# Splitting the first loads of a DCN cross network over three DMA queues

## The chip, the cores and the metric

The kernel runs on one core of one Trainium2 chip. The metric is the device time of one execution in microseconds (us), lower is better; the time before is the median of 3 runs.

## The reference

Six layers of a cross network over a batch of 4096 rows with 416 features, all in bfloat16:

```python
B, F, D, L = 4096, 26, 16, 6
Din = min(F * D, 1024)            # 416
# x0: (B, Din), ws: (L, Din, Din), bs: (L, Din)
def reference(x0, ws, bs):
    x = x0
    for l in range(ws.shape[0]):
        x = x0 * (x @ ws[l] + bs[l]) + x
    return x
```

## The kernel before

The batch is worked on in four blocks of 1024 rows (index `s`), each through six layers (index `l`). Inside a block everything is transposed: features lie on the partitions, rows on the free axis. The 416 features are three full chunks of 128 (`c`, `m`, `k`) and a tail of 32. The block's 1024 columns are two halves of 512 (`h`), so that layer `l` of half 0 can leave PSUM while half 1 is being multiplied. The sum over layers is not added by a vector engine: the products of all layers of a block pile up in the same PSUM banks, since x of layer l is x0 times (1 + the sum so far), and the running bias sum `cb_sb` takes the place of the bias.

For each layer TensorE does, in this order: the main matmuls of half 0 (`main`, 36 matmuls of 128 x 32 weights by 512 columns, four of them beside each other in the array), the tail's contribution to the three chunks and to the tail itself (`tail_rows`, which uses the weights `wt_sb` and, for the tail by tail corner of 32 x 32, the tile `wc_sb`), the contribution of the chunks to the tail (`tail_outs`), and the main matmuls of half 1. VectorE takes each finished bank to bfloat16 (`leave`, L429, six in every layer). The tail goes through ScalarE (L439), a multiplication on GpSimd (L452) and four copies that swap quarters, two on ScalarE (L416) and two on GpSimd (L418).

The corner tile `wc_sb` is zero but for 32 x 32 blocks. It is set to zero once (L272, GpSimd), and `corner` (L274) copies the blocks out of `wt_sb` on GpSimd: layer 0's before the loops (L541), layer 1's after the first layer's tail (L571), those of layers 2 to 5 after the second's (L573).

The start is written out by hand. Fourteen matmuls on constants (`fill`, L293) run while the first rows are loaded. The first half of block 0, four tiles of 128 rows (`xin_sb`), is transposed on TensorE with the identity `ident` (L500), two tiles and one chunk at a time, and copied from PSUM by VectorE (L515, chunks 0 and 2) and ScalarE (L510, chunk 1) into `x0T_sb`. The second half of block 0 comes by a transposing DMA (`load_transposed`, L205), like the later blocks. Layer 0's first half runs chunk by chunk (`k` outermost), so that each chunk of its weights W0 is needed only when its turn comes; in between stand the bias sums (`bias_sums`, from the biases `bsa_sb` and the triangular mask `u_sb`) and the transposing of the tail's rows (`tail_in`, from `xin_sb` and `xtl_sb`).

The DMA queues are filled ahead of all else, in program order: SyncE issues rows 0 to 255, the three chunks of W0, the tail columns `xtl_sb`, the transposing load, W1, the tail weights of layer 1 (`wt1`), W2, the tail weights of layers 2 to 5 (`wt2`), W3 to W5, and the later blocks. ScalarE issues rows 256 to 511, the biases and layer 0's tail weights (`wt0`). GpSimd issues none.

A small planner (`Plan`) keeps, for each key such as `("w", 1)` or `("wc", ...)`, who wrote and who read it last, and turns that into semaphore waits. The order of instructions on an engine is the order in which they are added. GpSimd's copies that move data between partitions carry `shifts=True`, and the key `("shift",)` keeps them apart from GpSimd's other work.

Of the kernel before, what the change touches and what calls it, by code (L numbers as in the profile page):

```python
# [15 lines left out]
class Plan:  # L16
# [11 lines left out]
    def add(self, eng, fn, reads=(), writes=(), adds=(), parts=(), dma=None, shifts=False):  # L28
        if eng == "gpsimd" and dma is None:
            if shifts:  # L30
                adds = tuple(adds) + (("shift",),)
            else:
                reads = tuple(reads) + (("shift",),)
        op = Op()
        op.eng, op.fn, op.marked, op.dma, op.waits = eng, fn, False, dma, []
        needs = []
        for key in tuple(reads) + tuple(adds):
            needs += [(w, True) for w in self.writer.get(key, ())]
            if key[0] == "ps":
                needs += [(r, False) for r in self.readers.get(key, ())]  # L40
        for key in tuple(writes) + tuple(adds):
            needs += [(w, True) for w in self.writer.get(key, ())]
            needs += [(r, False) for r in self.readers.get(key, ())]
        for key in parts:
            needs += [(r, False) for r in self.readers.get(key, ())]
        clock = self.clock[eng]
        for need, raw in sorted(needs, key=lambda n: -n[0].idx):
            lane = need.group if need.dma else need.eng
            if dma and need.dma == dma:
                continue  # L50
            if need.dma is None and need.eng == eng and dma is None and (eng == "tensor" or not raw):
                continue
            if clock.get(lane, -1) >= need.idx:
                continue
            op.waits.append(need)
            need.marked = True
            for lane2, idx in need.clock.items():
                clock[lane2] = max(clock.get(lane2, -1), idx)
            clock[lane] = max(clock.get(lane, -1), need.idx)
        op.idx = len(self.ops[eng])  # L60
        op.group = None
        if dma:
            op.group = ("dma", dma)
            members = self.groups.setdefault(op.group, [])
            members.append(op)
            op.marked = True
        op.clock = dict(clock)
        self.ops[eng].append(op)
        for key in reads:
            self.readers.setdefault(key, []).append(op)  # L70
        for key in parts:
            if self.readers.get(key):
                self.writer[key], self.readers[key] = [], []
            self.writer.setdefault(key, []).append(op)
        for key in tuple(writes) + tuple(adds):
# [43 lines left out]
def bass_standalone__dcn_v2_cross__recsys_kernel(  # L119
# [6 lines left out]
    B, D = x0.shape  # L126
    L = ws.shape[0]
# [14 lines left out]
    with ExitStack() as es:  # L142
# [38 lines left out]
        def quad(q):  # L181
            return slice(32 * q, 32 * q + 32)
# [8 lines left out]
        def load_main(l):  # L191
            load(
                "sync", w_sb[:, l, :, :], ws[l, 0:DF, :].rearrange("(k p) n -> p k n", p=128), "w%d" % l, [("w", l)]
            )

        def load_rows(queue, i):
            load(queue, xin_sb[:, 2 * i:2 * i + 2, :], x0_v[:, 2 * i:2 * i + 2, :], "xin%d" % i, [("xin", i)])

        def load_tail_weights(a, b, name):
            for q in range(4):  # L200
# [25 lines left out]
                part(g, 0, 1)  # L226
                part(g, 1, 1)

        load_rows("sync", 0)
        load_rows("scalar", 1)  # L230
        for k in CH:
            load("sync", w_sb[:, 0, k, :], ws[0, 128 * k:128 * k + 128, :], "w0_%d" % k, [("w", 0, k)])
        load("scalar", bsa_sb[1:L + 1, :], bs[:, :], "bs", [("bs",)])
        load(
            "scalar", wt_sb[:, 0, :], ws[0, DF:D, :].unsqueeze(0).to_broadcast([4, DR, D]), "wt0", [("wt", "wt0")]
        )
        load("sync", xtl_sb[:, 4:JS, :], x0_v[:, 4:JS, DF:D], "xtl0", [("xtl", 0)])
        load_transposed(0, H, SB)
        load_main(1)
        load_tail_weights(1, 2, "wt1")  # L240
        load_main(2)
        load_tail_weights(2, L, "wt2")
# [3 lines left out]
        for s in range(1, NS):  # L246
# [16 lines left out]
            ), reads=[("ones",)], writes=[("ident",)],  # L263
        )
        P.add("gpsimd", lambda e: e.memset(bsa_sb[0:1, :], 1.0), writes=[("bs1",)])
        P.add(
            "gpsimd", lambda e: e.affine_select(
                out=u_sb[:, :], in_=ones_sb[0:L + 1, 0:L], pattern=[[1, L]],
                compare_op=ALU.is_ge, fill=0.0, base=1, channel_multiplier=-1,
            ), reads=[("ones",)], writes=[("u",)],  # L270
        )
        P.add("gpsimd", lambda e: e.memset(wc_sb[:, :, :, :], 0.0), writes=[("wc", "wt%d" % i) for i in range(3)])  # L272

        def corner(a, b, name):  # L274
            for g in range(4):
                p = quad(g | 1)
                P.add(
                    "gpsimd", lambda e, p=p, g=g: e.tensor_copy(  # L278
                        out=wc_sb[p, a:b, g % 2, quad(g)], in_=wt_sb[p, a:b, DF:D]
                    ), reads=[("wt", name), ("wc", name)], writes=[("wc", name, g)], shifts=True,  # L280
                )


# [47 lines left out]
        def tail_rows(s, l, start):  # L331
# [22 lines left out]
            def second(pe):  # L354
# [11 lines left out]

            P.add("tensor", first, reads=keys, adds=[("ps", bank(h, m)) for h in HALVES for m in range(2)])
            P.add(
                "tensor", second, reads=keys + [("wc", wkey(l), g) for g in range(4)],
                adds=[("ps", bank(h, 2)) for h in HALVES] + [("ps", T_BANK[h]) for h in HALVES],  # L370
            )

# [17 lines left out]
        def tail_in():  # L390
# [9 lines left out]
                            )  # L400
                return ins

            P.add("tensor", fn, reads=[("ident",), ("xtl", 0), ("xin", 0), ("xin", 1)], adds=[("ps", 7)])
# [86 lines left out]

        HEAD_BANKS = ((3, 4, 5), (6, 2, 7))
        B_BANK = 6
        fill(14)
        for i in range(2):
            for c in CH:
                b = HEAD_BANKS[i][c]

                def fn(pe, i=i, c=c, b=b):
                    for j in range(2):
                        ins = pe.transpose(  # L500
                            out=psT[:, b, j * 128:(j + 1) * 128],
                            in_=xin_sb[:, 2 * i + j, c * 128:(c + 1) * 128], identity=ident[:, :],
                        )
                    return ins

                P.add("tensor", fn, reads=[("xin", i), ("ident",)], adds=[("ps", b)])
                dst, src = x0T_sb[:, c, i * 256:(i + 1) * 256], psT[:, b, 0:256]
                if c == 1:
                    P.add(
                        "scalar", lambda e, d=dst, s=src: e.activation(out=d, in_=s, func=ACTF.Copy),  # L510
                        reads=[("ps", b)], writes=[("x0Tp", c, i)],
# [216 lines left out]
```

## Time and profile before

| | |
|---|---|
| median of 3 runs | 129.5 us (129.32 to 129.96) |
| profiled execution, own time | 130.31 us |
| its span | 128.7 us |
| TensorE (PE) busy | 124.5 us, 97% of the span |
| VectorE (DVE) busy | 98.3 us, 76% |
| ScalarE (ACT) busy | 44.3 us, 34% |
| GpSimd (POOL) busy | 39.6 us, 31% |
| W0, a third each (SyncE's queue) | 104 KB, landed 3.6 us after issue (median) |
| W1 to W5, each (SyncE's queue) | 312 KB, landed 4.4 us after issue (median) |

The span runs from the first to the last instruction of the profiled execution. PE is TensorE's matmul, PEld its weight load, DVE VectorE, ACT ScalarE, POOL GpSimd; SPq and ACTq are the DMA-issuing sides of SyncE and ScalarE. L285 is line 285 of the kernel; as it stands in the helper `mm`, nearly all matmuls carry it, and the tiles behind it tell them apart. In a timeline row the first number is the start in us, the second the length in us, and the brackets give the idle time before it and what ended it. Matmuls overlap in the array, so that steps between their starts say more than their lengths.

### The profile page before, as it was taken

How to read it: one execution, taken by the hardware profiler on the slowest of the kernel's cores; microseconds unless marked ns; L12 is line 12 of the kernel's file. 1: busy time of each engine (PE TensorE's matmuls, PEld its weight loads, DVE VectorE, ACT ScalarE, POOL GpSimd, SP SyncE). 2: the span in 40 equal slices, each digit the busy share in tenths (PEclk: the TensorE clock that was granted, in tenths of full speed). 3: DMA queues.
4: the chain of work that ended last, by engine and by line, in shares of the span. 5: the costliest groups of instructions: out<-in, count | busy, mean ns of one | idle time of the engine just before them, and what ended most of it. 6: DMA issues, size and time to landing. Idle time of an engine off the chain costs nothing.

```text
span 128.7 us, 5290 instructions
## 1 busy us (share of the span) xinstructions
PE 124.5 (97%) x2402; PEld 64.5 (50%) x2402; DVE 98.3 (76%) x150; ACT 44.3 (34%) x97; POOL 39.6 (31%) x88
## 2 busy tenths in 40 slices
PE   7998999999999999999999999999999999999991
PEld 5553545545545545545545545545455455455660
DVE  0319489698797797797797797797797797797973
ACT  1525233343313243252222252252222252253920
POOL 7024273142122243242221251341320341440550
PEclk9999999999999999999999999999999999999999
DMA  3987999019999994500009407200008906100017
GB/s 110 198 203 184 265 210 231 21 37 233 195 177 240 172 166 157 156 8 5 0 5 189 81 0 248 63 5 0 0 5 167 103 5 216 54 0 5 0 38 232
DMA packets 34998, 14.11 MB, mean 110 GB/s; under 512 B 25690, under 2 KB 34976, under 8 KB 34976
## 3 DMA queue, kind: packets, MB, share of 16 engines
q1 hardware_dynamic: 34272, 13.24, 49.3%
q10 hardware_dynamic: 704, 0.54, 1.3%
q8 instruction: 19, 0.31, 1.0%
q14 instruction: 3, 0.02, 0.2%
HBM read 3.87 MB, written 3.41 MB: 57 GB/s over the span
## 4 chain that ended last, share of the span: by engine, by line
PE 88%; SPq 4%; DMA 4%; DVE 0%; issue 0%
PE ps L285 88%; DMA w_sb<-in_ws_dram 4%; SPq L205 2%; SPq L189 2%; DVE o_sb L659 0%
## 5 line engine op out<-in xcount | busy, mean ns | idle before, releaser
L429 DVE SCALAR_TENSOR_TENSOR xT_sb<-ps,cb_sb,x0T_sb 128x512 bf16<-128x512 f32 x120 | 80.9, 743 | 20.3 <-PE ps L285 20.3
L285 PE MATMUL ps<-xT_sb,w_sb 128*32 128x512 bf16 (+1 forms) x1596 | 84.2, 364 | 0.6 <-DMA w_sb<-in_ws_dram 0.6
L285 PEld LDWEIGHTS ps<-xT_sb,w_sb 128*32 128x32 bf16 x1596 | 40.8, 97 | 38.1 <-issue 4.0
L439 ACT ACTIVATE t_sb<-ps,cb_sb 64x256 f32<-64x256 f32 x46 | 21.6, 469 | 57.7 <-PE ps L285 57.4
L452 POOL TENSOR_TENSOR xt_sb<-t_sb,x0t_sb 128x256 bf16<-128x256 f32 x20 | 13.4, 672 | 63.4 <-ACT t_sb L439 63.4
L416 ACT ACTIVATE xt_sb<-xt_sb 32x256 bf16<-32x256 bf16 x38 | 15.7, 414 | 15.4 <-POOL xt_sb L452 15.2
L285 PE MATMUL ps<-x0T_sb,w_sb 128*32 128x512 bf16 (+1 forms) x336 | 19.3, 373 | 0.0
L418 POOL COPY xt_sb<-xt_sb 32x256 bf16<-32x256 bf16 x38 | 14.9, 392 | 2.4
L429 DVE SCALAR_TENSOR_TENSOR xo_sb<-ps,cb_sb,x0T_sb 128x512 bf16<-128x512 f32 x18 | 12.1, 744 | 2.5 <-PE ps L285 2.5
L285 PEld LDWEIGHTS ps<-x0T_sb,w_sb 128*32 128x32 bf16 x336 | 8.4, 98 | 7.6 <-issue 0.8
L285 PE MATMUL ps<-xt_sb,wt_sb 32*128 32x512 bf16 (+1 forms) x152 | 11.7, 326 | 0.0
L285 PE MATMUL ps<-xt_sb,wc_sb 32*128 32x256 bf16 x76 | 7.4, 268 | 0.0
L285 PEld LDWEIGHTS ps<-xt_sb,wt_sb 32*128 32x128 bf16 x152 | 2.4, 91 | 8.3 <-DVE xT_sb L429 6.4
L452 POOL TENSOR_TENSOR xot_sb<-t_sb,x0t_sb 128x256 bf16<-128x256 f32 x3 | 2.0, 672 | 9.9 <-ACT t_sb L439 9.9
L285 PE MATMUL ps<-w_sb,xT_sb 128*32 128x416 bf16 (+1 forms) x60 | 5.1, 339 | 0.0
L278 POOL COPY wc_sb<-wt_sb 32x32 bf16<-32x32 bf16 (+1 forms) x12 | 2.8, 233 | 5.1 <-DMA wt_sb<-in_ws_dram 4.5
L659 DVE TENSOR_TENSOR o_sb<-ps,xr_sb 128x416 bf16<-128x416 f32 x6 | 3.4, 587 | 1.3 <-PE ps L285 1.0
L293 PE MATMUL ps<-const-bfloat16-1.0 128*128 128x256 bf16 x14 | 3.1, 415 | 0.8 <-PEq L713 0.8
L285 PEld LDWEIGHTS ps<-xt_sb,wc_sb 32*128 32x128 bf16 x76 | 3.8, 93 | 0.2
L515 DVE COPY x0T_sb<-ps 128x256 bf16<-128x256 bf16 x4 | 1.1, 292 | 3.5 <-PE ps L500 3.2
L461 ACT ACTIVATE sS_sb<-ps,cb_sb 128x512 bf16<-128x512 f32 x5 | 3.0, 692 | 0.0
L285 PEld LDWEIGHTS ps<-w_sb,xT_sb 128*32 128x32 bf16 (+1 forms) x60 | 2.3, 97 | 1.4 <-issue 0.2
(39 smaller groups left out, 28.8 us busy)
## 6 DMA issues: line engine op xcount, KB each, us to landing
out_dram<-o_sb SPq DMA_DIRECT2D x3, 832.0 KB, 4.2
w_sb<-in_ws_dram SPq DMA_DIRECT2D x5, 312.0 KB, 4.4
xr_sb<-in_x_dram SPq DMA_DIRECT2D x1, 832.0 KB, 6.3
wt_sb<-in_ws_dram SPq DMA_DIRECT2D x4, 104.0 KB, 2.9
out_dram<-o_sb SPq DMA_DIRECT2D x2, 208.0 KB, 2.2
w_sb<-in_ws_dram SPq DMA_DIRECT2D x3, 104.0 KB, 3.6
xin_sb<-in_x_dram SPq DMA_DIRECT2D x1, 208.0 KB, 3.0
xin_sb<-in_x_dram ACTq DMA_DIRECT2D x1, 208.0 KB, 3.3
```

Source lines behind the costliest of these rows:

```text
L189: P.add(queue, lambda e: e.dma_start(dst, src), writes=writes, dma=name)
L205: "sync", lambda e: e.dma_start_transpose(x0T_sb[:, :, s * SB + a:s * SB + b], x0[s * SB + a:s * SB + b, 0:DF]),
L278: "gpsimd", lambda e, p=p, g=g: e.tensor_copy(out=wc_sb[p, a:b, g % 2, quad(g)], in_=wt_sb[p, a:b, DF:D]), reads=[("wt", name), ("wc", nam ...
L285: return pe.matmul(dst, lhsT=lhsT, rhs=rhs, start=start, stop=True, skip_group_check=True, tile_position=pos,)
L293: ins = pe.matmul(ps[:, 7, 0:256], lhsT=const[:, 0:128], rhs=const, start=True, stop=True)
L416: fn = lambda e, d=dst, s=src: e.activation(out=d, in_=s, func=ACTF.Copy)
L418: fn = lambda e, d=dst, s=src: e.tensor_copy(out=d, in_=s)
L429: "vector", lambda e: e.scalar_tensor_tensor(out=dst, in0=ps[:, bank(h, c), :], scalar=cb_sb[:, c, l:l + 1], in1=x0T_sb[:, c, o:o + H], op ...
L439: "scalar", lambda e, p=p, h=h: e.activation(out=dst[p, :], in_=ps[p, T_BANK[h], 0:G], func=ACTF.Identity, bias=cb_sb[p, NC, l:l + 1]), re ...
L452: "gpsimd", lambda e: e.tensor_tensor(out=dst, in0=t, in1=x0t_sb[:, s, 0, :], op=ALU.mult),
L461: fn = lambda e: e.activation(out=o, in_=i, func=ACTF.Identity, bias=b)
L659: "vector", lambda e: e.tensor_tensor(out=o_sb[:, jj, :], in0=ps[:, b, 0:D], in1=xr_sb[:, j, :], op=ALU.mult), reads=[("ps", b), ("xr",)], ...
```

## The change

The rows 0 to 255 become two loads of one tile each on SyncE's queue, and the start transposes tile by tile, with 12 fill matmuls and not 14. Of the first pair of tiles VectorE now copies all three chunks; of the second, ScalarE still copies chunk 1. The third chunk of W0 and all of W1 move to ScalarE's queue. The biases are loaded by GpSimd's queue. The corner blocks of layers 1 to 5 are loaded from memory by four DMAs on GpSimd's queue, each 32 partitions by 5 layers by 32 elements, and the copies after layers 0 and 1 go; layer 0's corner is still copied by GpSimd. The zeros of `wc_sb` are written by VectorE. In the planner, a shifting GpSimd copy now also waits for GpSimd's own earlier readers of the `("shift",)` key.

```diff
-            needs += [(r, False) for r in self.readers.get(key, ())]
+            needs += [(r, key == ("shift",)) for r in self.readers.get(key, ())]
...
-        load_rows("sync", 0)
-        load_rows("scalar", 1)
+        load_rows("sync", 0, 1)
+        load_rows("scalar", 2, 4)
+        load_rows("sync", 1, 2)
         for k in CH:
-            load("sync", w_sb[:, 0, k, :], ws[0, 128 * k:128 * k + 128, :], "w0_%d" % k, [("w", 0, k)])
-        load("scalar", bsa_sb[1:L + 1, :], bs[:, :], "bs", [("bs",)])
+            load(
+                ("sync", "sync", "scalar")[k], w_sb[:, 0, k, :], ws[0, 128 * k:128 * k + 128, :], "w0_%d" % k, [("w", 0, k)]
+            )
         load(
             "scalar", wt_sb[:, 0, :], ws[0, DF:D, :].unsqueeze(0).to_broadcast([4, DR, D]), "wt0", [("wt", "wt0")]
         )
+        load_main(1, "scalar")
         load("sync", xtl_sb[:, 4:JS, :], x0_v[:, 4:JS, DF:D], "xtl0", [("xtl", 0)])
         load_transposed(0, H, SB)
-        load_main(1)
         load_tail_weights(1, 2, "wt1")
...
         P.add("gpsimd", lambda e: e.memset(bsa_sb[0:1, :], 1.0), writes=[("bs1",)])
+        P.add("gpsimd", lambda e: e.dma_start(bsa_sb[1:L + 1, :], bs[:, :]), writes=[("bs",)], dma="bs")
...
-        P.add("gpsimd", lambda e: e.memset(wc_sb[:, :, :, :], 0.0), writes=[("wc", "wt%d" % i) for i in range(3)])
-
-        def corner(a, b, name):
+        P.add("vector", lambda e: e.memset(wc_sb[:, :, :, :], 0.0), writes=[("wc",)])
+        for g in range(4):
+            P.add(
+                "gpsimd", lambda e, g=g: e.dma_start(
+                    wc_sb[quad(g | 1), 1:L, g % 2, quad(g)], ws[1:L, DF:D, DF:D].rearrange("l p n -> p l n")
+                ), reads=[("wc",)], writes=[("wc1",)], dma="wc",
+            )
+
+        def corner():
             for g in range(4):
                 p = quad(g | 1)
                 P.add(
-                    "gpsimd", lambda e, p=p, g=g: e.tensor_copy(
-                        out=wc_sb[p, a:b, g % 2, quad(g)], in_=wt_sb[p, a:b, DF:D]
-                    ), reads=[("wt", name), ("wc", name)], writes=[("wc", name, g)], shifts=True,
+                    "gpsimd", lambda e, p=p, g=g: e.tensor_copy(out=wc_sb[p, 0, g % 2, quad(g)], in_=wt_sb[p, 0, DF:D]),
+                    reads=[("wt", "wt0"), ("wc",)], writes=[("wc0", g)], shifts=True,
                 )
...
-                "tensor", second, reads=keys + [("wc", wkey(l), g) for g in range(4)],
+                "tensor", second, reads=keys + ([("wc1",)] if l else [("wc0", g) for g in range(4)]),
...
-        fill(14)
-        for i in range(2):
+        fill(12)
+        for j in range(4):
+            i, r = divmod(j, 2)
             for c in CH:
                 b = HEAD_BANKS[i][c]
-
-                def fn(pe, i=i, c=c, b=b):
-                    for j in range(2):
-                        ins = pe.transpose(
-                            out=psT[:, b, j * 128:(j + 1) * 128],
-                            in_=xin_sb[:, 2 * i + j, c * 128:(c + 1) * 128], identity=ident[:, :],
-                        )
-                    return ins
-
-                P.add("tensor", fn, reads=[("xin", i), ("ident",)], adds=[("ps", b)])
+                P.add(
+                    "tensor", lambda pe, j=j, r=r, c=c, b=b: pe.transpose(
+                        out=psT[:, b, r * 128:(r + 1) * 128], in_=xin_sb[:, j, c * 128:(c + 1) * 128], identity=ident[:, :]
+                    ), reads=[("xin", j), ("ident",)], adds=[("ps", b)],
+                )
+                if r == 0:
+                    continue
                 dst, src = x0T_sb[:, c, i * 256:(i + 1) * 256], psT[:, b, 0:256]
-                if c == 1:
+                if i and c == 1:
                     P.add(
...
-        corner(0, 1, "wt0")
+        corner()
...
-                if s == 0 and l == 0:
-                    corner(1, 2, "wt1")
-                if s == 0 and l == 1:
-                    corner(2, L, "wt2")
```

More of the change, by code (lines that the diff above doesn't have):

```diff
@@ L189, in load, with load_main, load_rows @@
             P.add(queue, lambda e: e.dma_start(dst, src), writes=writes, dma=name)
-        def load_main(l):
+        def load_main(l, queue="sync"):
             load(
-                "sync", w_sb[:, l, :, :], ws[l, 0:DF, :].rearrange("(k p) n -> p k n", p=128), "w%d" % l, [("w", l)]
+                queue, w_sb[:, l, :, :], ws[l, 0:DF, :].rearrange("(k p) n -> p k n", p=128), "w%d" % l, [("w", l)]
             )
-        def load_rows(queue, i):
-            load(queue, xin_sb[:, 2 * i:2 * i + 2, :], x0_v[:, 2 * i:2 * i + 2, :], "xin%d" % i, [("xin", i)])
+        def load_rows(queue, a, b):
+            load(queue, xin_sb[:, a:b, :], x0_v[:, a:b, :], "xin%d" % a, [("xin", j) for j in range(a, b)])
         def load_tail_weights(a, b, name):
@@ L401, in fn @@
                 return ins
-            P.add("tensor", fn, reads=[("ident",), ("xtl", 0), ("xin", 0), ("xin", 1)], adds=[("ps", 7)])
+            P.add("tensor", fn, reads=[("ident",), ("xtl", 0), ("xin", 0), ("xin", 1), ("xin", 2), ("xin", 3)], adds=[("ps", 7)])
             P.add(
```

## The prediction, made before the change was run

> **What bounds the kernel now.** I read the chain that ended last first, then the waits of the first 20 us, then the timeline of the start. The chain, in order of time (start us, length us, what):
>
> ```profile
> 3.49 3.18 SPq L205
> 6.66 0.05 issue
> 6.71 5.47 DMA w_sb<-in_ws_dram
> 12.18 0.04 issue
> 12.22 113.84 PE ps L285 x2160
> ```
>
> From 12.22 us on the end is set by TensorE alone. Before that the chain is one transfer: layer 1's main weights (W1), issued on SyncE's queue at 6.71, behind the transposing load whose issue holds that queue for 3.18 us. The waits up to 20 us (us in total, times, longest) name the places where TensorE stood still:
>
> ```profile
> PEld ps L285 <- DMA w_sb<-in_ws_dram: 1.1, 1, 1.1
> ...
> PEld ps L285 <- POOL wc_sb L278: 0.7, 2, 0.4
> ...
> PE ps L285 <- DMA w_sb<-in_ws_dram: 0.6, 1, 0.6
> ```
>
> How much each costs is read from the corner matmuls (wc_sb), which come once in every layer. The first of them is in the timeline of the start (start us, length us), the others in that of 12 to 30 us:
>
> ```profile
> 0.82 3.15 PE L293 MATMUL ps<-const-bfloat16-1.0 128*128 128x256 bf16 x14 [0.82 <-PEq L713]
> ...
> 3.81 1.46 PE L500 MATMUL ps<-ident,xin_sb 128*128 128x128 bf16 x12
> 4.24 1.36 DVE L515 COPY x0T_sb<-ps 128x256 bf16<-128x256 bf16 x4 [3.19 <-PE ps L500]
> ...
> 5.23 1.47 PE L285 MATMUL ps<-x0T_sb,w_sb 128*32 128x512 bf16 x12
> ...
> 6.83 0.83 PE L285 MATMUL ps<-x0T_sb,w_sb 128*32 128x512 bf16 x12
> ...
> 7.01 1.00 POOL L278 COPY wc_sb<-wt_sb 32x32 bf16<-32x32 bf16 x4 [3.76 <-DMA wt_sb<-in_ws_dram]
> ...
> 8.82 0.27 PE L285 MATMUL ps<-x0t_sb,wc_sb 32*128 32x256 bf16 x1
> ...
> 9.14 2.45 PE L285 MATMUL ps<-x0T_sb,w_sb 128*32 128x256 bf16 x48
> ```
>
> ```profile
> 14.52 0.27 PE L285 MATMUL ps<-xt_sb,wc_sb 32*128 32x256 bf16 x1
> ...
> 19.54 0.28 PE L285 MATMUL ps<-xt_sb,wc_sb 32*128 32x256 bf16 x1
> ...
> 24.42 0.27 PE L285 MATMUL ps<-xt_sb,wc_sb 32*128 32x256 bf16 x1
> ...
> 29.30 0.27 PE L285 MATMUL ps<-xt_sb,wc_sb 32*128 32x256 bf16 x1
> ```
>
> The steps are 5.70, 5.02, 4.88 and 4.88 us, and 4.88 holds for all later layers. So TensorE's own pace is 4.88; layer 0 to 1 loses 0.82 us (the wait for W1), layer 1 to 2 loses 0.14 us (the corner copies of layers 2 to 5 on GpSimd). The rest of the span hangs on one number, the 8.82 us at which layer 0 reaches its first corner matmul.
>
> **The change part by part.**
>
> *W1 to ScalarE's queue.* ScalarE's queue now issues two row tiles (0.50 us, its row), the third chunk of W0 (0.43 to 0.46, SyncE's rows), wt0 (0.64) and W1 (0.57): from 0.79 to about 3.1, where today three issues end at 2.63. The activation table load behind them (1.28) and the dummy activation (0.21) shift by 0.45 to end near 4.65; ScalarE's first real copy is now that of the second row pair, ready at about 4.85. Nothing waits. W1 is issued 4.2 us earlier; with its 5.47 us it would land by 8.0, against a need at about 11.4. The 0.82 goes in full if nothing is late next: the next input is layer 0's third VectorE result of the first half, which ends by 9.05 + 3 x 0.74 = 11.3. So -0.8. SyncE's later issues move up by the 0.6 us of W1's issue: wt1, W2 and wt2, which by the landing records were in at 13.0, 13.6 and 15.3, will be needed at about 13.4, 16 and 18.2. wt1 has the least room, 0.4 us today and up to 1.0 then; that gains nothing and keeps the 0.82 whole.
>
> *Corners of layers 1 to 5 by DMA.* GpSimd loses eight copies (1.00 and 1.34 us for four) behind which TensorE waited at 19.2: -0.14. The memset of wc_sb (1.37 us on GpSimd) goes to VectorE: between GpSimd's 1.37 and twelve times VectorE's 0.165 us memset of 128 elements, 2.0; from 1.05 it ends by 3.05, and VectorE is idle until its first copy at about 4.1. Cover 1.0 us, cost nothing. Two further edits are free: bias sums need the bias row at 6.6 us, and the added wait of a shifting GpSimd copy for earlier GpSimd work only names instructions that precede it in order; its queue holds nothing that TensorE needs sooner.
>
> *Five DMAs issued by GpSimd.* No row of this trace has one. GpSimd's order becomes: identity (to 1.41), ones row (to 1.80), bias DMA, the small mask (0.18), four corner DMAs that wait for VectorE's memset, then the four layer 0 copies (1.00), which wait for wt0 (7.0 today). What is queued behind the DMAs is thus layer 0's corner, and TensorE waits for it at 8.82. The nearest rows are other queues' issues: 0.42 the shortest, 0.62 for this very bias load on ScalarE's queue, 1.46 the longest of a plain load. At 0.62 they are over at 5.5 and the copies start with wt0 as now; at 1.46 they end at 3.4 + 5.84 = 9.3, the copies at 10.3, and TensorE stands 1.5 us. The break is at 1.17 us each (3.0 + 4 x 1.17 + 1.0 = 8.7). I take the bias row, 0.62: nothing, bounds 0 and +1.5. DMA: Bandwidth & Descriptors of the Trainium skill (Latency and other measured facts) gives about 1 us for a GpSimd DMA's software descriptors against 0.6 on the other queues. By it the DMAs would end near 7.0 and the copies near 8.0: still no loss, with 0.7 us to spare, and no run here shows it.
>
> *Rows as tiles 0 and 1 apart, 12 fill matmuls.* Fills take 0.213 us each, so twelve end near 3.38 and not 3.80. The first tile's 104 KB should be there (208 KB landed 3.0 us after issue, at 3.8), the second tile at 3.8 as before. TensorE then does tile 1's transposes from about 3.75, and the first VectorE copy starts near 4.1 instead of 4.24. But VectorE now copies three blocks of the first pair before the first block of the second (0.292 each): 4.1 + 4 x 0.295 = 5.28, and the first main matmuls need that block; they start at 5.23 today. The 0.4 us that the transposes come earlier is thus lost in VectorE's queue: +0.05, between -0.2 (if tile 1 lands with tile 0's gain) and +0.3 (if it lands late).
>
> *What W1 collides with.* 312 KB enter the queues next to wt0, xtl and the transposing load of the second half. In 3 to 4 us the windows show 330 GB/s, so W1 is 0.95 us of all engines. The transposing load landed 5.1 us after 3.49, at 8.6; the matmuls at 9.14 wait for it. Pushed by 0 to 0.95 it lands at 8.6 to 9.55, a stall of 0 to 0.45. The share from 4 to 5 us is only 0.57, so part of W1 falls into idle time: I take +0.2. xtl has the same risk with smaller size (its matmuls were issued 0.2 us after it landed) and stands inside that figure.
>
> Sum against the profiled execution (span 128.7, own time 130.31, so 1.6 around it): -0.82 - 0.14 + 0.05 + 0.2 = -0.7, a span of 128.0 and 129.6 in all. That execution is 0.8 above the median of the runs shown, so the difference goes onto the median: 129.5 - 0.7 = **128.8**.
>
> **The rivals.**
>
> *Slower, by GpSimd's DMAs.* If one costs over 1.17 us, layer 0's corner is late, and each 0.1 us more costs 0.4. At 1.46 us the sum is -0.96 + 0.05 + 1.5 = +0.6, 130.1; at 1.6, 130.7. For it: no row bounds a GpSimd issue, and four in a row stand ahead of a due copy. Against it: all rows of that size of transfer are near half of 1.17. Chance 0.22.
>
> *Slower, by TensorE's clock.* The 12 matmuls at 5.23 take 1.47 us, the same 12 at 6.83 take 0.83: the speed doubles near 6.8, though the granted-clock row reads full throughout. With the transposes ending at about 4.7 and the main matmuls at 5.28, TensorE now idles 0.5 us where it idled under 0.2. If that puts the step off beyond layer 0's first half, the 1.5 us from 6.83 to 8.37 double: -0.96 + 0.05 + 1.5 = +0.6, 130.1. TensorE: Matmul & The Clock Gate of the Trainium skill (Part 1) speaks against this change: the clock is released after a window of about 3.4 us of sustained activity. By it a missed window would cost up to half of 3.4 us, an estimate from the page. Against: two thirds of the stretch stay busy. Chance 0.10.
>
> *No change: the wait for W1 is not there in the timed runs, or is given back.* The trace's landing records have 15 of W1's 16 parts in by 9.9 us and one at 12.18, with a 16 KB instruction fetch (queue q8) at 9.83 between them. The profiled execution lies 0.8 above the median, just the size of that wait. Without it: -0.14 + 0.25 = +0.1, 129.6. The same end follows if the transposing load is late by all of its bound and xtl too. Against: the fetch follows TensorE's instruction count, which the timed runs share. Chance 0.16.
>
> **How the numbers follow.** Forecast (W1's wait gone, head within 0.3 us of before): 0.52, own range 128.4 to 129.2. About 0.5% is what a measurement of this kernel can tell from no change: below 128.85 is faster, above 130.15 slower. Of the forecast's 0.52, 0.44 lie below 128.85 and 0.08 above; the third rival's 0.16 is no change; of the slower pair's 0.32, 0.31 is slower and 0.01 no change. Faster 0.44, same 0.25, slower 0.31. The range of 8 in 10 reaches from 128.2 (both collisions nil, head 0.2 better gives 128.3) to 130.5, between the rivals' 130.1 and 130.7.
>
> **What would show it.** Right: the step from the first to the second corner matmul falls from 5.70 to 4.9 to 5.1, the next from 5.02 to 4.88, W1 no longer in the chain, the first corner matmul at 8.7 to 9.2. GpSimd's DMA rows under 1.17 us and TensorE waiting for wc_sb nowhere speak for the first step; a wait of TensorE on GpSimd's wc_sb at 8.8 or later is the first rival; 12 main matmuls still taking 1.4 us after 7 us is the second. The forecast is wrong if the first corner matmul comes after 9.5, whatever holds it, or if a changed kernel that has both steps at 4.88 still takes 129.4.

## The result, and the profile after

The changed kernel takes 130.64 us (median of 7, 130.24 to 131.17); before, in the same comparison, 129.48 us. The ratio is 1.0106, interval 1.0072 to 1.0140: slower by 1.1%. The forecast was faster, 128.8 us, and the time lies just outside its range (128.2 to 130.5). In some of the kernels below a few executions lie more than 1.5% above the kernel's fastest; the medians and ratios leave these out.

The chain that ended last in the changed kernel, in order of time (start us, length us, what):

```profile
3.19 0.04 issue
3.24 7.66 DMA x0T_sb<-in_x_dram
10.90 0.04 issue
10.95 115.96 PE ps L293 x2208
```

W1 is out of the chain, as forecast. In its place stands the transposing load of block 0's second half: issued at 3.24, landed at 10.9, where it landed at 8.6 before. The waits of the first 20 us (us in total, times, longest) show that this is the last of several:

```profile
PEld ps L293 <- DMA w_sb<-in_ws_dram: 0.6, 1, 0.6
...
PE ps L293 <- DMA w_sb<-in_ws_dram: 0.5, 1, 0.5
...
PEld ps L293 <- DMA x0T_sb<-in_x_dram: 0.3, 1, 0.3
```

And the timeline of the start tells them in order (start us, length us):

```profile
2.68 2.35 POOL L278 DMA_DIRECT2D wc_sb<-in_ws_dram  x4
...
5.39 0.83 PE L293 MATMUL ps<-x0T_sb,w_sb 128*32 128x512 bf16 x12 [0.53 <-DVE x0T_sb L521]
...
6.91 1.39 PE L293 MATMUL ps<-x0T_sb,w_sb 128*32 128x512 bf16 x12 [0.50 <-DMA w_sb<-in_ws_dram]
...
8.33 0.29 PE L293 MATMUL ps<-ident,xin_sb 128*32 128x128 bf16 x2
...
8.71 1.52 PE L293 MATMUL ps<-x0T_sb,w_sb 128*32 128x512 bf16 x12
...
10.51 0.27 PE L293 MATMUL ps<-x0t_sb,wc_sb 32*128 32x256 bf16 x1
...
10.95 2.45 PE L293 MATMUL ps<-x0T_sb,w_sb 128*32 128x256 bf16 x48
```

The second chunk of W0 landed at 6.87 (5.39 before) and the matmuls at 6.91 had stood 0.50 us for it. xtl landed at 8.19 (7.05 before); here TensorE did not stand for it, since the matmuls ahead of the tail's transposes ran until 8.30. The first corner matmul comes at 10.51 and not at 8.82, and half 1's matmuls, at 10.95 and not at 9.14, stood for the transposing load. After that all is as forecast. TensorE's rows of 14 to 26 us:

```profile
15.51 0.27 PE L293 MATMUL ps<-xt_sb,wc_sb 32*128 32x256 bf16 x1
...
20.39 0.27 PE L293 MATMUL ps<-xt_sb,wc_sb 32*128 32x256 bf16 x1
```

The steps are 5.00 and 4.88, where they were 5.70 and 5.02. In sum, 1.69 us were lost ahead of the first corner matmul and 0.84 won behind it; that makes the span's 129.6 for 128.7.

Most of the 1.69 us is the clock, and still the time does not hang on it. The windows of this execution (stretch, its length, busy time of PE, PEld, DVE, ACT and POOL, granted clock, DMA share, GB/s):

```profile
4.00:5.00 1.00, 0.68 (x9) 0.51 (x9) 0.55 (x3) 0.99 (x3) 1.00 (x2) 1.00 0.88 159
5.00:6.00 1.00, 0.61 (x12) 0.23 (x12) 0.54 (x3) 0.23 (x1) 0.04 (x1) 1.00 0.96 261
6.00:7.00 1.00, 0.50 (x27) 0.26 (x24) 0.00 (x0) 0.19 (x1) 0.00 (x0) 1.00 2.47 238
7.00:8.00 1.00, 1.00 (x12) 0.20 (x12) 0.00 (x0) 0.00 (x0) 0.20 (x2) 0.52 0.61 77
...
9.00:10.00 1.00, 1.00 (x12) 0.18 (x4) 0.00 (x0) 0.59 (x1) 0.00 (x0) 0.50 1.23 269
```

TensorE had been busy for only 50 to 68% of each microsecond from 4 to 7 us, and from 7.04 to 10.45 it was granted half its clock: the twelve matmuls at 6.91 took 1.39 us and those at 8.71 took 1.52, where twelve take 0.82 or 0.83 at full clock. That is 3.41 us, the window that the Trainium skill states in TensorE: Matmul & The Clock Gate (Part 1) as about 3.4 us; here the two agree.

At full clock TensorE would have stood for xtl instead. Run 2 below, at full clock, has its first corner 1.48 us after xtl; from 8.19 that makes about 9.7, an estimate. Half 1 would still have waited for the transposing load until 10.90. And the other six executions, whose mean granted clock was 0.999 or 1.0, took 130.24 to 131.17 us, with this one's 131.05 among them. The lowered clock is not the cause of the 1.1%.

Outside the span the two kernels differ as well: the time less the span is 1.51 us in the changed kernel's executions and 1.26 us in the 31 of before in the first experiment. More on that below.

### The profile page after: what moved, and what is told of

It is laid out like the page before. It is cut to its first block, busy times and chain, and to the rows that moved or that the text cites. A ratio compares the mean times of both kernels' runs of the same rounds, so it can differ in the third digit from the quotient of the medians.

```text
span 129.6 us, 5277 instructions
## 1 busy us (share of the span) xinstructions
PE 124.6 (96%) x2400; PEld 64.2 (50%) x2400; DVE 99.0 (76%) x152; ACT 43.8 (34%) x96; POOL 39.4 (30%) x84
## 3 DMA queue, kind: packets, MB, share of 16 engines
HBM read 3.91 MB, written 3.41 MB: 57 GB/s over the span
## 4 chain that ended last, share of the span: by engine, by line
PE 90%; DMA 6%; SPq 2%; DVE 0%; issue 0%
PE ps L293 90%; DMA x0T_sb<-in_x_dram 6%; SPq L189 2%; DVE o_sb L661 0%
## 5 line engine op out<-in xcount | busy, mean ns | idle before, releaser
L293 PE MATMUL ps<-x0T_sb,w_sb 128*32 128x512 bf16 (+1 forms) x336 | 19.9, 381 | 1.1 <-DVE x0T_sb L521 0.5
L437 DVE SCALAR_TENSOR_TENSOR xo_sb<-ps,cb_sb,x0T_sb 128x512 bf16<-128x512 f32 x18 | 12.1, 744 | 2.5 <-PE ps L293 2.5
L672 POOL TENSOR_TENSOR o_sb<-f_sb,xr_sb 128x416 bf16<-128x416 f32 x2 | 1.9, 976 | 2.9 <-ACT f_sb L668 2.9
```

Of the source, the lines that this page charges most:

```text
L293: return pe.matmul(dst, lhsT=lhsT, rhs=rhs, start=start, stop=True, skip_group_check=True, tile_position=pos,)
L437: "vector", lambda e: e.scalar_tensor_tensor(out=dst, in0=ps[:, bank(h, c), :], scalar=cb_sb[:, c, l:l + 1], in1=x0T_sb[:, c, o:o + H], op ...
L672: "gpsimd", lambda e: e.tensor_tensor(out=o_sb[:, jj, :], in0=t, in1=xr_sb[:, j, :], op=ALU.mult),
```

## The experiments

Two theories stood at the start. **W**: W1's 312 KB, now ahead of xtl and the transposing load in time, make these late. **C**: the corner DMAs of GpSimd do. "First corner" is the start of layer 0's first corner matmul, "span" the mean over a kernel's executions. Each comparison has its own runs of before, with medians between 129.13 and 129.28 us.

**1. The changed kernel with W1 back on SyncE's queue**

```diff
-        load_main(1, "scalar")
...
         load_transposed(0, H, SB)
+        load_main(1)
```

> The changed kernel with W1 back on SyncE's queue, in its old place behind the transposing load; all else as changed. Theory W (W1's 312 KB run beside xtl and the transposing load and make them late): the first corner matmul, 8.8 us before and 10.5 us after, comes back to 8.8 to 9.2, the step to the second is again 5.5 to 5.8 because W1 is late, time about 129.5 us. Theory C (the four corner DMAs of GpSimd make them late): the first corner matmul stays at 10.2 or later and W1 is late as well, time 131 us or more.

Measured: 130.24 us, ratio 1.0067 (1.0037 to 1.0098); first corner 9.24. W1 landed at 10.7 and nothing waited for it. The first step was 5.46, but TensorE stood there for the transposing load, which landed at 10.1. W is half right: the first corner comes back, to just above the expected 8.8 to 9.2, and the rest of the change costs 0.7% without W1. With the corner DMAs alone the transposing load lands at 8.85 (run 4), with the third chunk and the biases alone at 8.3 (run 13); what makes it late when they come together was not tried apart.

**2. The changed kernel with the corners copied as before**

```diff
-                "gpsimd", lambda e, g=g: e.dma_start(wc_sb[...], ws[1:L, DF:D, DF:D]...)
...
+                if s == 0 and l == 0:
+                    corner(1, 2, "wt1")
+                if s == 0 and l == 1:
+                    corner(2, L, "wt2")
```

> The changed kernel with the corners of layers 1 to 5 copied by GpSimd as before, no corner DMAs; the bias DMA stays on GpSimd's queue and W1 on ScalarE's. Theory W: first corner matmul stays at 10.2 to 10.6, the second step is again 5.0, time 130.6 to 130.9 us. Theory C: first corner matmul at 8.8 to 9.2, first step 4.9 to 5.0, time about 128.8 us.

Measured: 130.67 us, ratio 1.0104 (1.0064 to 1.0145); first corner 10.02, second step 5.01. As theory W expected it. TensorE's rows:

```profile
8.68 0.23 PE L288 MATMUL ps<-ident,xin_sb 128*32 128x128 bf16 x2 [1.10 <-DMA xtl_sb<-in_x_dram]
...
10.02 0.27 PE L288 MATMUL ps<-x0t_sb,wc_sb 32*128 32x256 bf16 x1
```

The transposing load landed at 9.97, where it landed at 10.90 with the corner DMAs; in the times they are worth nothing either way.

**3. Before, with W1 alone on ScalarE's queue**

```diff
         load("scalar", wt_sb[:, 0, :], ...)
+        load_main(1, "scalar")
...
-        load_main(1)
```

> The kernel before with one part of the change alone: W1 is issued on ScalarE's queue after wt0. Theory W: first corner matmul at 9.8 to 10.5, first step 4.9 to 5.0, time 129.9 to 130.6 us. Theory C: first corner matmul 8.8 to 9.1, time 128.6 to 128.9 us.

Measured: 130.35 us, ratio 1.0077 (1.0045 to 1.0109), span 128.9 for 128.0; first corner 9.35, first step 4.88. This is theory W, and the largest single part of the loss. The start of its chain that ended last (further on the chain has a transposing DMA of the ninth step, which loses 0.66 us; see the last section):

```profile
2.76 5.20 DMA xtl_sb<-in_x_dram
7.96 0.04 issue
8.00 0.44 PE ps L285 x16
```

**4. Before, with the corner DMAs alone**, and the planner's edit that goes with them

```diff
-        P.add("gpsimd", lambda e: e.memset(wc_sb[:, :, :, :], 0.0), ...)
+        P.add("vector", lambda e: e.memset(wc_sb[:, :, :, :], 0.0), writes=[("wc",)])
+        for g in range(4):
+            P.add("gpsimd", lambda e, g=g: e.dma_start(wc_sb[...], ...), ...)
```

> The kernel before with one part of the change alone: corners of layers 1 to 5 by four GpSimd DMAs, zeros by VectorE; biases and W1 where they were. Theory W: first corner matmul 8.8 to 9.0, second step 4.88, time about 129.4 us. Theory C: first corner matmul 9.8 or later, xtl landed after 8 us, time 130.4 us or more.

Measured: 129.61 us, ratio 1.0037 (0.9996 to 1.0079); first corner 8.66, second step 4.88, xtl landed at 7.2. The 0.14 us of the corner copies is won where it was forecast, theory C finds nothing in the landings, and the time is still not better (mean span 128.3 for 128.0).

**5. Before, with the row split alone.** By now the split was under suspicion (theory R).

```diff
-        load_rows("sync", 0)
-        load_rows("scalar", 1)
+        load_rows("sync", 0, 1)
+        load_rows("scalar", 2, 4)
+        load_rows("sync", 1, 2)
...
-        fill(14)
+        fill(12)
```

> The kernel before with the row split alone: tiles 0 and 1 as two loads, transposes tile by tile, 12 fills, three VectorE copies for the first pair. Theory R (the split starts layer 0 later, since tile 1 lands only at 4.1 us and VectorE has three copies ahead of the block that is needed): the first main matmuls start at 5.4 to 5.7 and not 5.0 to 5.3, span 0.3 to 0.5 us longer, time 129.6 to 129.8 us against 129.3. Its rival, that the split is neutral and W1 and the corners carry all: span within 0.1 us of before.

Measured: 129.23 us, ratio 1.0017 (0.9987 to 1.0047), span 127.9 as before. Tile 1 landed at 4.0 and the main matmuls started at 5.47, as theory R has it, yet the span did not grow: what TensorE needs next (xtl, at 7.2) was no later. R falls. Outside the span stood 1.47 us for 1.25.

**6. The changed kernel without the row split**

```diff
-        load_rows("sync", 0, 1)
-        load_rows("scalar", 2, 4)
-        load_rows("sync", 1, 2)
+        load_rows("sync", 0)
+        load_rows("scalar", 1)
...
-        fill(12)
+        fill(14)
```

> The changed kernel without the row split: rows 0 to 255 as one load, 14 fills, ScalarE copies chunk 1 of both pairs; W1, the third chunk, biases and corners stay as changed. Theory R: main matmuls again from 5.0 to 5.3, span about 0.4 us shorter than the changed kernel's 129.1, time 130.2 to 130.3 us. Rival: 130.6 us as the changed kernel.

Measured: ratio 1.0202 (1.0138 to 1.0265), from two executions of 131.42 and 132.40 us. Neither theory had it: without the split the kernel is about a further 1% slower. The execution that was profiled took 133.62 us; in it TensorE stood 2.94 us for the transposing load, and 3.41 us at half clock followed. Its chain that ended last:

```profile
2.76 9.32 DMA x0T_sb<-in_x_dram
12.08 0.04 issue
12.12 117.56 PE ps L292 x2202
```

One load fewer on SyncE's queue puts the transposing load's issue at 2.76 and not at 3.24, ahead of W1's (3.01 on ScalarE's queue). The two then run side by side with the corner packets from the start, and landed at 12.1 and 11.4. That the order of the issues does it is a reading; run 15 shows the same late landing in an execution of 131.22 us.

**7. Before, with xtl alone on ScalarE's queue**

```diff
+        load("scalar", xtl_sb[:, 4:JS, :], ..., "xtl0", [("xtl", 0)])
         load("scalar", bsa_sb[1:L + 1, :], ...)
...
-        load("sync", xtl_sb[:, 4:JS, :], ..., "xtl0", [("xtl", 0)])
```

> The kernel before with one load moved: the tail columns xtl go from SyncE's queue, behind W0, to ScalarE's, behind its row tiles. If TensorE's wait for xtl is what the late start costs, xtl lands at 5 to 6 us and not at 7 to 8, the matmuls on it never wait, and the time falls by up to 0.4 us, to 128.9 to 129.2. If the transposing load or wt0 is next in line at the same place, nothing is gained: 129.2 to 129.5 us.

Measured: 129.24 us, ratio 1.0002 (0.9969 to 1.0035). xtl landed at 4.6 and the first corner came at 8.15, the earliest of all; the span was 127.8 for 127.9, and outside it stood 1.51 us for 1.25. In the profiled execution 0.47 us of the gain went again in the ninth step.

**8. Before, unchanged, once more**

> The kernel before, unchanged, in another profiled execution. If the late landing of W1 (12.18 us, one part of sixteen) belongs to the kernel, the first step between corner matmuls is again 5.5 to 5.8 us. If it belonged to that one execution, W1 lands by 10.2 us, the step is 4.9 to 5.1 and the span about 128.0 us, where two kernels with W1 in its old place (the changed kernel with W1 back, and before with the corner DMAs) had it at 10.7 and 9.9 us.

Measured: 129.7 us, span 128.4. TensorE's rows of the first 20 us:

```profile
8.69 0.27 PE L285 MATMUL ps<-x0t_sb,wc_sb 32*128 32x256 bf16 x1
...
13.57 0.27 PE L285 MATMUL ps<-xt_sb,wc_sb 32*128 32x256 bf16 x1
...
18.61 0.28 PE L285 MATMUL ps<-xt_sb,wc_sb 32*128 32x256 bf16 x1
```

The first step is 4.88: all sixteen parts of W1 had landed by 9.85. The wait of 0.82 us on which the forecast stood is in one of the two traced executions of before. In eight more variants of the kernel before that have W1 in its old place and the corner copies (runs 5, 7, 9, 11, 12, 13, 16 and 17) the step is 4.88 or 4.89 too. The instruction fetch is there in run 8 as well, from 9.62 to 10.56, and W1 is not late; what held one part until 12.18 in the first execution stays open.

**9 to 12. Spreading wt0, and swapping xtl with the biases.** wt0 is one load whose source is repeated four times. Its landing leaves one record at 3.1 us, which must stand for 12 of the 16 completion counts, and four from 6.6 to 6.9, so its packets seem to run on 4 of the 16 DMA engines. DMA: Bandwidth & Descriptors of the Trainium skill (Rules for kernel authors) says that a leading broadcast of c copies confines a load to at most c engines; the four late records agree. The packet records show what goes on in the transposing load, whose 1,536 packets of 256 bytes no other load of the start has. In run 8 they start at 4.92 us, and some 440 have ended by 6.75. Eighteen that start from 5.75 to 6.38 are held for more than 0.4 us and end together, at 6.97 to 7.01; only then do the rest run, at about 1,100 packets per us. In run 3 the held packets start from 6.30 and end at 7.7; in the changed kernel they start from 6.28 and end at 8.3 to 8.4. Theory B: the load is held until the slowest engine has worked off what is queued ahead. Rival S: the bytes alone count.

```diff
-        load("scalar", wt_sb[:, 0, :], ws[0, DF:D, :].unsqueeze(0).to_broadcast([4, DR, D]), "wt0", [("wt", "wt0")])
...
+        for q in range(4):
+            load("gpsimd", wt_sb[quad(q), 0, :], ws[0, DF:D, :], "wt0", [("wt", "wt0")])
```

Run 9, before with this alone:

> The kernel before with one load changed: wt0, one broadcast load on ScalarE's queue whose packets run on 4 of the 16 DMA engines, becomes four loads of 32 partitions on GpSimd's queue. Theory B (the transposing load is held at its first packet on all engines until the slowest engine has worked off what is queued ahead, and wt0's four engines are the slowest): the held packets end at 5.8 to 6.3 us and not at 7.0, xtl lands by 6.4, the transposing load by 7.9, first corner matmul at 8.1 to 8.4, span about 0.3 us shorter than before. Rival S (all loads share the engines' bandwidth and it is the sum of bytes that counts): the same bytes, so xtl at 7.0 to 7.3 and the transposing load at 8.5 to 8.8 as before, span unchanged.

Measured: 129.10 us, ratio 0.9975 (0.9946 to 1.0004). Eleven packets are still held that long, but only to 6.37; xtl landed at 6.6, the transposing load at 8.0, first corner 8.22. B in the trace; in the time a gain of 0.2% that could be none. The chain that ended last holds no DMA any more:

```profile
7.29 0.61 ACT x0t_sb L404
7.90 0.05 issue
7.95 116.71 PE ps L284 x2216
```

Run 10, W1 on ScalarE's queue (as run 3) with wt0 spread:

> Before with W1 on ScalarE's queue (which alone made the span 0.8 us longer) and wt0 by four loads on GpSimd's queue. Theory B: W1 no longer stands behind wt0 on four engines; held packets end by 7.0 us, xtl lands by 7.2, the transposing load by 8.7, first corner matmul by 8.7, span 0.5 to 0.8 us shorter than with W1 alone, about 128.1. Rival S: xtl at about 7.9, transposing load at about 9.3, span about 128.9 as with W1 alone.

Measured: 130.35 us, ratio 1.0079 (1.0053 to 1.0105), span 128.8: no better than W1 alone. The held packets end at 7.37, xtl landed at 7.7, the transposing load at 8.9, but now wt0 came at 8.15 and layer 0's corner copies held TensorE. That speaks for S: with wt0 spread, W1's bytes make something else late.

Run 11, xtl on ScalarE's queue and the biases on SyncE's, in xtl's place:

> The kernel before with xtl on ScalarE's queue behind the row tiles and the biases on SyncE's queue in xtl's place, so that each queue has as many loads as before. xtl lands at about 4.6 us as in the earlier run with xtl moved, first corner matmul about 8.2, span 127.6 to 127.8. If the 0.25 us that run spent outside its span comes from the number of loads on ScalarE's queue, it is gone here and the time is 128.9 to 129.0; if not, 129.1 to 129.2.

Measured: 129.44 us, ratio 1.0017 (0.9984 to 1.0051). The biases landed at 7.1, TensorE stood for them, first corner 9.3. In both orders the small load behind W0 on SyncE's queue is the late one.

Run 12, runs 9 and 11 together:

> Both: wt0 by four loads on GpSimd's queue and xtl and biases swapped. Theory B: held packets end before 6 us, the transposing load lands by 7.5, first corner matmul 8.0 to 8.3, no wait for xtl; span 127.4 to 127.6, time 128.6 to 128.9 us, the best of all. Rival S: as the swap alone.

Measured: 129.71 us, ratio 1.0025 (0.9999 to 1.0050); biases at 6.8, wt0 at 7.2, first corner 9.12. Worse than either idea promised.

**13. Before, with the third chunk on ScalarE's queue and the biases on GpSimd's**

```diff
-            load("sync", w_sb[:, 0, k, :], ...)
-        load("scalar", bsa_sb[1:L + 1, :], ...)
+            load(("sync", "sync", "scalar")[k], w_sb[:, 0, k, :], ...)
...
+        P.add("gpsimd", lambda e: e.dma_start(bsa_sb[1:L + 1, :], bs[:, :]), writes=[("bs",)], dma="bs")
```

> The kernel before with the last part alone: the third chunk of W0 on ScalarE's queue, the biases on GpSimd's. With W1 back on SyncE's queue the changed kernel still took 0.7% more than before, while the row split alone gave +0.2% and the corner DMAs alone +0.4%. If the parts add, this one is worth 0.0 to 0.2%: span 127.9 to 128.2 us, xtl at 7.0 to 7.3. If the third chunk, queued ahead of wt0, is what is left, xtl lands at 7.5 to 7.9, span 128.3 to 128.5.

Measured: 129.74 us, ratio 1.0038 (1.0013 to 1.0064); span 128.2 for 128.0, outside it 1.51 us. In the profiled execution, one of 130.92 us that lost 1.41 in the ninth step, the biases landed at 6.62 and TensorE stood 0.87 us for them; xtl was not late (6.9). In the changed kernel's own trace the biases landed at 5.15, and nothing waited for them. With this each part has been run alone: rows 0.2%, corners 0.4%, W1 0.8%, this one 0.4%; they sum to 1.7%, together they cost 1.1%. The mean spans nearly add up: -0.05, +0.28, +0.82 and +0.20 make +1.25 us, and together they are +1.12 (129.16 in the changed kernel's seven executions, 128.04 in the 31 of before). What does not add is the time outside the span, longer by 0.23, 0.06, 0.23 and 0.24 us in the four alone and by 0.25 together.

**14. The changed kernel with W1 issued later on ScalarE's queue**

```diff
-        load_main(1, "scalar")
...
+        load_main(1, "scalar")
         for c in CH:
             P.writer[("x0T", 0, c, 0)] = ...
```

> The changed kernel with W1 still on ScalarE's queue, but issued behind the copies of the start, at about 5.3 us and not at 3.0. If W1's place in time is the cause (its packets run ahead of xtl and of the transposing load's first packets), xtl lands 0.4 us earlier or more (by 7.8), span falls by 0.4 us to about 128.7, time to about 130.2. If it is the queue that counts, whatever the time, nothing changes: 130.6 us.

Measured: 130.61 us, ratio 1.0102 (1.0062 to 1.0142). Issued at 5.28, W1 leaves xtl alone (landed at 7.0, first corner 8.50), and runs beside the transposing load instead. The chain that ended last:

```profile
3.24 6.78 DMA x0T_sb<-in_x_dram
10.01 0.04 issue
10.06 115.96 PE ps L292 x2208
```

TensorE stood 1.17 us for it, the first step was 6.12, and the time is that of the changed kernel. So the early issue alone does not do it: what W1 does from another queue while the transposing load is under way, it does not do from SyncE's own, behind that load. Nor is it the held packets here: they end at 6.7, and the load's last packet at 7.87, earlier than in run 8 (8.15). But its completion counts come from 9.64 to 10.01, right behind W1's (9.42 to 9.80), 1.8 to 2.1 us after that last packet; in run 8 this takes 0.3 to 0.5 us. Neither B nor S says why.

**15. The changed kernel with xtl on ScalarE's queue**

```diff
         load_rows("scalar", 2, 4)
+        load("scalar", xtl_sb[:, 4:JS, :], ..., "xtl0", [("xtl", 0)])
...
-        load("sync", xtl_sb[:, 4:JS, :], ..., "xtl0", [("xtl", 0)])
```

> The changed kernel with xtl on ScalarE's queue, right behind its row tiles. If the wait for xtl is the first thing that W1 makes late, xtl lands before 5 us, TensorE does not wait for it, and the span falls by 0.3 to 0.9 us. If the transposing load behind it is late all the same (10 to 11 us), TensorE waits there and the span stays within 0.2 us of the changed kernel's 129.1.

Measured: ratio 1.0200 (1.0127 to 1.0273), from two executions with spans of 129.9 and 131.1. xtl landed at 4.6, and the transposing load, issued 0.6 us earlier, at 11.3. A miss, and the second sight of what run 6 shows. The chain that ended last:

```profile
2.66 8.64 DMA x0T_sb<-in_x_dram
11.30 0.04 issue
11.35 115.96 PE ps L293 x2208
```

**16. A version meant to beat both**: runs 7 and 9 together.

> A version meant to beat both: the kernel before with wt0 by four loads on GpSimd's queue (alone 0.25% faster, interval touching none) and xtl on ScalarE's queue ahead of the biases, which stay there (in the other order the biases came late, at 6.8 us, and TensorE waited for them). xtl lands by 4.8 us, the biases by 5, the transposing load by 8.0, first corner matmul 8.0 to 8.3, span 127.4 to 127.7, time 128.7 to 129.0 us. If the loads on GpSimd's queue make wt0 late (7.2 us and more), the corner is next in line and the time stays at 129.1.

Measured: 129.94 us, ratio 1.0063 (1.0034 to 1.0093). xtl at 4.8, the biases at 5.3, the transposing load at 8.3, but wt0 only at 8.1. TensorE's rows:

```profile
8.23 0.40 PE L284 MATMUL ps<-x0t_sb,wt_sb 32*128 32x512 bf16 x6 [0.35 <-DMA wt_sb<-in_ws_dram]
9.29 0.39 PE L284 MATMUL ps<-x0t_sb,wt_sb 32*128 32x512 bf16 x1 [0.66 <-POOL wc_sb L277]
```

**17 and 18. wt0 first on GpSimd's queue; and corner copies one layer at a time**

```diff
+        for q in range(4):
+            load("gpsimd", wt_sb[quad(q), 0, :], ws[0, DF:D, :], "wt0", [("wt", "wt0")])
         load_rows("sync", 0)
...
-                if s == 0 and l == 0:
-                    corner(1, 2, "wt1")
-                if s == 0 and l == 1:
-                    corner(2, L, "wt2")
+                if s == 0 and l < L - 1:
+                    corner(l + 1, l + 2, wkey(l + 1))
```

Both also zero the corner tile on VectorE and carry the planner's edit. Run 17, without the second hunk:

> The kernel before with wt0 by four loads at the very head of GpSimd's queue (they stood behind the identity before, and wt0 landed at 6.9 to 8.1 us) and the zeros of the corner tile by VectorE. If wt0's late landing is what kept the spread load from paying, wt0 lands by 6.3 us, layer 0's corner copies end by 7.4, xtl by 6.5 and the transposing load by 8.0, first corner matmul 7.9 to 8.2, span 127.4 to 127.6, time 128.6 to 128.9 us. If GpSimd's packets wait behind the other queues whenever they are issued, wt0 lands at 6.9 or later as before and the time is 129.1.

Measured: 129.17 us, ratio 0.9997 (0.9970 to 1.0024). wt0's four loads were issued from 1.33 to 3.04 and landed at 4.6, 5.2, 5.8 and 7.2; the last was issued 0.44 us earlier than in run 9 and landed no earlier (7.0 there).

Run 18, with both:

> The same, and the corner copies of layers 2 to 5 made one layer at a time, one layer ahead, where they were four layers at once (1.34 us, then TensorE waits). The second step between corner matmuls falls from 5.02 to 4.88 and the later ones stay at 4.88: 0.14 us less than the run without this, 128.5 to 128.8 us.

Measured: 129.00 us, ratio 0.9999 (0.9970 to 1.0028). The second step is 4.88 from here on, with no DMA for it:

```profile
13.50 0.27 PE L284 MATMUL ps<-xt_sb,wc_sb 32*128 32x256 bf16 x1
...
18.38 0.27 PE L284 MATMUL ps<-xt_sb,wc_sb 32*128 32x256 bf16 x1
```

No version was found that is faster than before beyond its interval.

## Why the prediction was wrong, step by step

- **W1's wait, -0.82 us: the step that failed.** It was read correctly off the profiled execution, and the kernel does not have it every time: run 8 has W1 at 9.85 and a step of 4.88, and eight variants have that step too. The prediction named this as its third rival, on the right grounds (one part of sixteen was late, and the execution lay 0.8 us above the median), and gave it 0.16. Its argument against, that the timed runs share the fetch, did not hold: run 8 shares it, without the wait.
- **What W1 collides with, +0.2 us: mis-sized, and its bounds too.** They were taken from W1's bytes, 0 to 0.95 us on the transposing load. In the changed kernel that load came 2.3 us later and xtl, called the smaller risk, 1.1 us later. With W1 alone (run 3) the first corner is at 9.35 against 8.69 in run 8, +0.66, and the mean span is 0.82 longer. What the bound left out shows in two places: the load's packets are held together longer (to 7.7 in run 3, 7.0 in run 8), and its counts come later after its last packet (run 14). What does either is not shown.
- **The corner copies, -0.14 us: right.** The second step fell to 4.88 in the changed kernel and in run 4; run 18 shows that it needed no DMA.
- **GpSimd's DMAs: right.** They took 0.76 us for the biases and 0.57 to 0.64 each for the corners, near the 0.62 that was taken and far from the 1.17 at which layer 0's corner would be late. The 1 us that the prediction set beside this from the page is stated there for the first byte of a transfer, not for the time that GpSimd is held. The first rival, the one given most on the slower side, had no part in it.
- **The row split, +0.05 us: right in its sum** (run 5: span 0.05 shorter), though tile 1 landed at 4.0 to 4.1 and not 3.8.
- **The clock** did step down in the profiled execution, as the second rival feared, for 3.41 us, after TensorE had stood 0.53 us before the first main matmuls and 0.50 for W0's second chunk. It did not in the other six executions, and here the transposing load was later still.
- **The third chunk and the biases, costed at nothing: wrong.** Alone they cost 0.4% (run 13), 0.2 us of it in the span. The prediction took the bias load's landing for granted; in run 13 it came at 6.62, later than TensorE needed it, but in the changed kernel at 5.15. Which of the two moves costs is not shown.
- **Time outside the span, taken as unchanged:** 1.26 us before, 1.51 us after, about 0.25 of the 1.4 us between the medians of the changed kernel and of before in run 1's comparison. What sets it is open. It was about 1.5 in every execution of runs 2, 3, 7, 10, 13, 14 and 16 and 1.2 to 1.3 in those of runs 6, 9, 12, 15 and 17; in runs 1, 4, 5, 11 and 18 executions of about 1.25 stand beside others of 1.6 to 1.9. The number of loads on ScalarE's queue, the guess that run 11 was to test, does not order them (run 13 has three, as before, and run 6 four).

Put together, as an estimate from the parts alone: the span was forecast to fall by 0.71 us and rose by 1.12, a gap of 1.83. W1's wait is 0.82 of it, the collision 0.62 (0.82 for 0.2), the corners 0.42 (+0.28 for -0.14, a cost that is not clear of none), the third chunk and the biases 0.20, the row split -0.10; that makes 1.96. So the slower side came about by a mechanism that the prediction had among its terms, as a nuisance of 0.2 us, and among its rivals only as a second way to no change.

## What to carry to other kernels

A wait in one profiled execution is a term of the sum only if the kernel has it every time: where one part in sixteen lands 2 us late and the execution lies above the median by just that wait, profile again, or cost the edit without it. A load that is moved to an emptier queue gained a place in time here at the expense of the loads that it had stood behind; ask of each of those when it is needed, and keep what is needed late on the queue of what is needed early, behind it. Bytes over bandwidth was no bound for a transposing load beside another queue's load: 0.95 us by the sum, 2.3 us in the changed kernel.

## What the runs showed of the hardware that was not expected

- Some way into the transposing load, eleven to twenty of its packets are held for more than 0.4 us and released together: at 6.4 us in run 9, at 7.0 in run 8, at 7.7 with W1 beside it (run 3), at 8.3 to 8.4 in the changed kernel. Held by the slowest engine is a reading that runs 3, 8 and 9 agree with; the packet records do not name the engine, so it is not shown.
- The load's landing can come long after its last packet: 0.3 to 0.5 us in run 8, 0.6 to 1.2 in the changed kernel, 1.8 to 2.1 in run 14, where W1's packets run until 8.96. Of the eighteen runs 1, 4, 6, 14, 15 and 16 go beyond 0.7 us. In these and in the changed kernel, and in no others, a load of ScalarE's or GpSimd's queue landed only after that last packet. What makes the counts wait is open.
- Run beside W1 and the corner packets from its start, the same load landed 8.6 to 9.3 us after its issue (runs 15 and 6), where it took 5.1 in run 8 and 6.9 with the corner packets beside it and W1 behind it (run 1).
- Half a clock does not need a TensorE that stands still. It followed 3.42 us in which TensorE was busy for 2.03 us, 59% (changed kernel, from 3.62); after 3.41 us with 2.29 us busy, 67% (run 13, from 3.93), and with 2.41, 71% (run 10, from 4.41), the clock stayed full.
- Seven of the twenty traces lose 0.2 to 1.4 us in one later place, the ninth step (5.1 to 6.3 for 4.88). GpSimd's copy for the first block's store waits there for a transposing DMA and stands ahead of the tail's own work, as in run 8's GpSimd rows:

```profile
51.09 0.40 POOL L480 COPY o_sb<-ot_sb 128x256 bf16<-128x256 bf16 x1 [4.58 <-DMA ot_sb<-xot_sb]
51.45 0.68 POOL L452 TENSOR_TENSOR xt_sb<-t_sb,x0t_sb 128x256 bf16<-128x256 f32 x1
```

A start that is won by some tenths can be lost again there; that was not tried apart.
